# Order of the last two gate/value chunks of each batch in a fused attention and GeGLU kernel

## The chip, the cores and the metric

The kernel runs on one core of a Trainium2 chip. The metric is the device time of one execution in microseconds (us); lower is better. The time before is the median of three runs, 366.04 us (366.04 to 366.19). Matmuls run on TensorE (PE in the profile; its weight loads are PEld), elementwise work on VectorE (DVE), activation functions on ScalarE (ACT), masks and most DMA issues on GpSimd (POOL), and the stores and DMA transposes are issued by SyncE (SP). Matmul results land in PSUM[...].

## The reference: what is computed

In outline: causal attention over 8 batches, 8 heads, 576 positions and 64 dimensions, with 16 "beacon" keys that every position sees; its output, with the heads side by side, goes through a gated feed-forward block.

```python
k_all = np.concatenate([beacon_k, k], axis=2)          # 16 + 576 keys
scores = scale * np.matmul(q, k_all.transpose(0, 1, 3, 2))
scores = np.where(causal, -1e9, scores)
a = softmax(scores)
x = np.matmul(a, v_all)                                # -> x[4608, 512]
g, val = x @ w_gate, x @ w_val                         # 512 -> 1536
out = (gelu(g) * val) @ w_out                          # 1536 -> 512
```

Inputs and output are float32; the kernel computes in bfloat16 with float32 accumulation.

## The kernel before

The work is written out by hand, in program order, as one loop over the batches `b`. The feed-forward block works on chunks of 512 rows of x; chunk `b` is computed in the pass of batch `b`, and there are nine chunks, the ninth after the loop. Every engine runs its instructions in the order in which they are written.

A pass of batch `b` has two stages. In the **attention stage** the kernel computes scores of batch `b` in pieces, `scores(b, (m, c), ...)` with `m` the pair of heads and `c` one of four pieces of the triangle of keys and queries; each call fills one PSUM buffer, then ACT takes the exponential of it into SBUF, and POOL zeroes the masked corner (L320). `av` and `av_head` multiply the exponentials by v, `normalize` divides on DVE. Between these, `o(n)` puts the next `n` units of the output product of chunk `b-1`. For `b` above 1 the first twelve units are `out_half_mms`: each unit is two matmuls of 64 contraction rows, on the two halves of the array, into two banks, and after the twelfth DVE copies one bank (L471) and adds the other (L472). The rest are `out_mms`, one matmul of 128 rows each, and one copy (L469) per twelve.

In the **gate/value stage** there are twelve pairs `fi`: four matmuls of 512 columns for the gate, four for the value, Gelu on ACT from the gate's bank into `ge_sb` (L171), and a product on DVE of `ge_sb` and the value's bank into `hT_sb` (L448). The output product of the next pass reads `hT_sb`. All matmuls are recorded at one line, L168, all activations at L171, so the trace tells them apart by tile: `gv_ps`, `g_ps` and `v_ps` for gates and values, `s_ps` for scores, `o_ps` for outputs, `x_ps` for attention times v.

PSUM is divided among three pools: `psum_s` has three buffers of two banks each, used in turn; `psum_t` and `psum_o` have one bank each. A pair `fi` takes one `psum_s` buffer, gate in one bank and value in the other. The last pair of a batch (`fi` = 11, for `b` below 7) is split: its gate is put in `psum_t`, Gelu follows it at once, and its value has a `psum_s` buffer. A score call takes the next `psum_s` buffer, so the first three score calls of a pass take the buffers of the pairs 9, 10 and 11 of the pass before, each when its DVE product is done. The two banks of the half output product are `psum_t` and `psum_o`. In batch 0, after the pairs 4, 6 and 8, `transpose_wide` transposes q and k of batch 1 on PE: k through `psum_t`, from which DVE copies (L218, then L222), and q through `psum_o`, from which ACT copies.

ACT switches its function tables twice per pass: the load before the exponentials stands at L616, the one before Gelu at L655.

Of the kernel before, what the change touches and what calls it, by code (L numbers as in the profile page):

```python
# [7 lines left out]
P = 128  # L8
B, H, S, NB, D = 8, 8, 576, 16, 64
# [4 lines left out]
F_TILES = D_FF // P  # L14
K_CHUNKS = D_MODEL // P
CH = 512
# [24 lines left out]
FP32 = mybir.dt.float32  # L41
BF16 = mybir.dt.bfloat16
ACT = mybir.ActivationFunctionType
ALU = mybir.AluOpType
# [5 lines left out]
def kernel(  # L50
# [12 lines left out]
    nc = tc.nc  # L63
    keep = tc.keep_in_program_order
# [6 lines left out]
    fpool = ctx.enter_context(tc.tile_pool(name="fpool", bufs=3))  # L71
    hpool = ctx.enter_context(tc.tile_pool(name="hpool", bufs=2))
    opool = ctx.enter_context(tc.tile_pool(name="opool", bufs=2))
    psum_s = ctx.enter_context(tc.tile_pool(name="psum_s", bufs=3, space=bass.MemoryType.PSUM))
    psum_t = ctx.enter_context(tc.tile_pool(name="psum_t", bufs=1, space=bass.MemoryType.PSUM))
    psum_o = ctx.enter_context(tc.tile_pool(name="psum_o", bufs=1, space=bass.MemoryType.PSUM))
# [6 lines left out]
    wg_sb = const.tile([P, K_CHUNKS, D_FF], BF16, name="wg_sb", tag="wg_sb")  # L83
    wv_sb = const.tile([P, K_CHUNKS, D_FF], BF16, name="wv_sb", tag="wv_sb")
    wo_sb = const.tile([P, F_TILES, D_MODEL], BF16, name="wo_sb", tag="wo_sb")
    xT_sb = const.tile([P, NPAIR, N_TOK + P - KROWS[4]], BF16, name="xT_sb", tag="xT_sb")
# [80 lines left out]
    def mm(out_ap, lhsT, rhs, start, stop, **kw):  # L167
        keep(nc.tensor.matmul(out_ap, lhsT, rhs, start=start, stop=stop, **kw))  # L168

    def act(out_ap, in_ap, func, **kw):  # L170
        keep(nc.scalar.activation(out_ap, in_ap, func, **kw))  # L171
# [17 lines left out]
    def transpose_pe(b, m, by_act=False):  # L189
        t_ps = psum_s.tile([P, 2, 1024], BF16, name="t_ps", tag="s")  # L190
        for w in range(2):
            tr_part(b, m, w, t_ps[:, w, :])
        out_ap = qkT[:, m, :, NB:SK].rearrange("p w (t r) -> p w t r", r=6)
        in_ap = t_ps[:, 0:2, 0:S].rearrange("p w (r t) -> p w t r", r=6)
        keep(nc.vector.tensor_copy(out_ap[:, 1], in_ap[:, 1]))
        if by_act:
            act(out_ap[:, 0], in_ap[:, 0], ACT.Copy)
        else:
            keep(nc.vector.tensor_copy(out_ap[:, 0], in_ap[:, 0]))
        keep(nc.vector.tensor_copy(qkT[:, m, 1, 0:NB], t_ps[:, 1, S:SK]))  # L200
# [59 lines left out]
    def scores(b, *parts):  # L260
        s_ps = psum_s.tile([P, 2, 512], FP32, name="s_ps", tag="s")
        c0 = 0
        for m, c in parts:
            score_mms(b, m, c, s_ps[:, :, c0 : c0 + CHUNK_W[c]])
            c0 += CHUNK_W[c]
        (m, c), n = parts[0], len(parts)
        o, w = CHUNK_OFF[c], CHUNK_W[c]
        act(
            exp_ring[:, m : m + n, :, o : o + w].rearrange("p g h c -> p h g c"),
            s_ps[:, :, 0 : n * w].rearrange("p h (g c) -> p h g c", g=n),  # L270
            ACT.Exp,
            scale=QK_SCALE,
        )
        if b:
            for m, c in parts:
                masks(b, m, c)
# [87 lines left out]
    def av(b, m):  # L364
        x = psum_s.tile([P, 2, 512], FP32, name="x_ps", tag="s")
        for hi in range(2):
            attend(b, m, hi, x[:, hi, :])
        normalize(b, m, x, 0, 2)

    def av_head(b, m, hi, pool, tag):  # L370
        x = pool.tile([P, 1, 512], FP32, name="x_ps", tag=tag)
        attend(b, m, hi, x[:, 0, :])
        normalize(b, m, x, hi, hi + 1)
# [10 lines left out]
    def turn_dma(b, m):  # L384
        y_sb, y_before = y_of[b * NPAIR + m], y_of.pop((b - 1) * NPAIR + m)
        keep(nc.vector.tensor_copy(y_sb[0:NB, 0, :, :], y_before[KROWS[4] - NB : KROWS[4], 4, :, :]))
        c0 = b * S - NB
        keep(
            nc.sync.dma_start_transpose(
                out=xT_sb[:, m, c0 : c0 + 5 * P].rearrange("p (j n) -> p j n", n=P),  # L390
                in_=y_sb.rearrange("p j e d -> p (j e d)"),
            )
        )
# [3 lines left out]
    def hold(b, m):  # L397
        x = xT_sb[:, m, b * S : (b + 1) * S]
        keep(nc.gpsimd.tensor_copy(hold_sb, x[:, 0 : S : S - 1]))  # L399
# [9 lines left out]
    h_of, o_of = {}, {}  # L409

    gv_of = {}

    def gv_mms(ci, fi, *kks, split=False, last=False):
        if (ci, fi) not in gv_of:
            if split:
                gv_of[ci, fi] = (
                    psum_t.tile([P, CH], FP32, name="g_ps", tag="t"),
                    psum_s.tile([P, 2, CH], FP32, name="v_ps", tag="s")[:, 0, :],
                )
            else:  # L420
                gv_ps = psum_s.tile([P, 2, CH], FP32, name="gv_ps", tag="s")
                gv_of[ci, fi] = (gv_ps[:, 0, :], gv_ps[:, 1, :])
        n0 = ci * CH

        def part(w):
            for kk in kks:
                mm(
                    gv_of[ci, fi][w],
                    (wg_sb, wv_sb)[w][:, kk, fi * P : (fi + 1) * P],
                    xT_sb[:, kk, n0 : n0 + CH],  # L430
                    kk == 0,
                    last and kk == kks[-1],
                    skip_group_check=True,
                )

        part(0)
        if not split:
            part(1)
        if not last:
            return  # L440
        ge_sb = fpool.tile([P, CH], BF16, name="ge_sb", tag="ge_sb")
        act(ge_sb, gv_of[ci, fi][0], ACT.Gelu)
        if split:
            part(1)
        if ci not in h_of:
            h_of[ci] = hpool.tile([P, F_TILES, CH], BF16, name="hT_sb", tag="hT_sb")
        keep(
            nc.vector.tensor_tensor(  # L448
                out=h_of[ci][:, fi, :], in0=gv_of.pop((ci, fi))[1], in1=ge_sb, op=ALU.mult
            )  # L450
        )

    def gate_val(ci, fi, split=False):
        gv_mms(ci, fi, *range(K_CHUNKS), split=split, last=True)

    def out_mm(ci, ti, fi, o_ps, c0=0, c1=D_MODEL):
        mm(
# [47 lines left out]
    def out_mms(ci, u0, u1):  # L505
        for u in range(u0, u1):
# [19 lines left out]
            out=eye,  # L526
# [25 lines left out]
    def ahead(n):  # L552
        for load in loads[:n]:
            load()
        del loads[:n]
# [52 lines left out]
    for b in range(B):  # L608
        u = [0]

        def o(n, halves=False):
            (out_half_mms if halves else out_mms)(b - 1, u[0], u[0] + n)
            u[0] += n

        if b:
            keep(nc.scalar.preload_act_table_set(SET_EXP))  # L616
            o(3, b > 1)
            scores(b, (0, 0))
            scores(b, (0, 2))
            scores(b, (0, 1))  # L620
            o(5 if b == 1 else 9, b > 1)
            if b == 1:
                transpose_pe(1, 3)
                o(5)
            ahead(2)
            scores(b, (0, 3), (1, 3))
            scores(b, (1, 0))
            scores(b, (1, 2))
            ahead(2)
            o(5 if b == 1 else 6)  # L630
            av_head(b, 0, 0, psum_t, "t")
            o(1)
            scores(b, (1, 1))
            scores(b, (2, 0))
            scores(b, (2, 2))
            ahead(2)
            av_head(b, 0, 1, psum_t, "t")
            turn_dma(b, 0)
            o(7)
            scores(b, (2, 1))  # L640
            scores(b, (2, 3), (3, 3))
            scores(b, (3, 0))
            av_head(b, 1, 0, psum_o, "o")
            o(5)
            av_head(b, 1, 1, psum_o, "o")
            turn_dma(b, 1)
            scores(b, (3, 1))
            scores(b, (3, 2))
            av(b, 2)
            turn_dma(b, 2)  # L650
            o(6)
            av(b, 3)
            turn_dma(b, 3)
            o(11)
            keep(nc.scalar.preload_act_table_set(SET_GELU))  # L655
            for kk in range(K_CHUNKS):
                for fi in range(2):
                    gv_mms(b, fi, kk, last=kk == 3)
        for fi in range(F_TILES):
            if fi >= 2:  # L660
                gate_val(b, fi, fi == F_TILES - 1 and b < B - 1)
            if b == 0 and fi in (4, 6, 8):
                transpose_wide(1, (fi - 4) // 2)
            if fi == 0:
                if b and b + 1 < B:
                    hold(b, 3)
                    load_v(b + 1)
                if b and b + 2 < B:
                    load_qk(b + 2)
                if 2 <= b + 1 < B:  # L670
                    transpose_dma(b + 1)
                store(nc.sync)
# [40 lines left out]
```

The softmax here doesn't subtract the row's maximum and nothing guards it: scores larger than these inputs give would overflow.

## Time and profile before

| | |
|---|---|
| median of three runs | 366.04 us |
| profiled execution: its time | 365.93 us |
| profiled execution: its span | 364.1 us |
| PE busy | 353.7 us, 97% of the span |
| ACT busy | 192.7 us, 53% |
| DVE busy | 162.8 us, 45% |
| POOL busy | 161.2 us, 44% |
| mean time of a 512-column matmul as recorded | 379 ns |

The span is what the trace covers; the execution's time has some 1.8 us around it. Matmuls overlap in the array, so a matmul recorded with 379 ns doesn't hold PE for that long: four of them of the kind `g_ps` start at 161.95 us and the next four at 162.82 us, a step of about 0.216 us. What a matmul costs is therefore read from the starts of those beside it. In the timeline, each row is a run of like instructions on one engine: start, length in us, engine, line, operation, tiles, shapes and count, and in brackets how long the engine stood idle ahead of it and what ended that.

The passes of the batches 2 to 6 repeat every 38.94 us (the `g_ps` matmuls start at 84.22, 123.17, 162.12, 201.06 in the chain).

### The profile page before, as it was taken

What the parts mean: (1) busy time and instruction counts of PE and PEld (TensorE: products, weight loads), DVE (VectorE), ACT (ScalarE), POOL (GpSimd) and SP (SyncE); (2) the same over time, 40 slices, a digit from 0 to 9 for tenths busy, and PEclk for the clock granted to TensorE, in tenths of its full rate; (3) what the DMA queues carried; (4) which work ended last, traced back from release to release, by engine and by line L of the source; (5) the groups of instructions that cost most, each with busy time, mean ns of one, the idle gap of its engine ahead of it and who ended that gap; (6) DMA issues with size and microseconds to landing.
All of it is one profiled execution on the core that took longest, in us unless ns stands there. A gap on an engine that the chain in (4) does not pass through costs nothing.

```text
span 364.1 us, 7726 instructions
## 1 busy us (share of the span) xinstructions
PE 353.7 (97%) x3164; PEld 184.8 (51%) x3206; DVE 162.8 (45%) x320; ACT 192.7 (53%) x252; POOL 161.2 (44%) x288
## 2 busy tenths in 40 slices
PE   7899999999999999999999999999999999999996
PEld 6665446444654455445644464446544564444443
DVE  4547836344443345434534354334444453333332
ACT  3975788237923594349623891379335953321210
POOL 8934497655537552945375455565330530000000
DMA  7999999899179945999299917991797253000102
GB/s 105 173 203 204 198 126 99 129 170 188 23 126 147 215 45 76 163 215 64 56 148 221 111 38 121 170 198 27 112 136 136 17 60 115 0 2 29 58 36 110
DMA packets 160419, 41.57 MB, mean 114 GB/s; under 512 B 146944, under 2 KB 155904, under 8 KB 160384
## 3 DMA queue, kind: packets, MB, share of 16 engines
q0 software_dynamic: 104848, 19.11, 68.9%
q1 hardware_dynamic: 55536, 21.96, 30.7%
q8 instruction: 25, 0.41, 0.5%
q14 instruction: 10, 0.08, 0.1%
HBM read 38.27 MB, written 9.44 MB: 131 GB/s over the span
## 4 chain that ended last, share of the span: by engine, by line
PE 80%; DMA 8%; POOL 6%; ACT 3%; issue 2%; DVE 0%; ACTq 0%; POOLq 0%
PE gv_ps L168 42%; PE o_ps L168 21%; PE x_ps L168 8%; PE s_ps L168 6%; DMA wo_sb<-in_moe_w_out_dram 4%; DMA qk<-in_q_dram 4%; ACT expT L171 3%; POOL qk L111 1%; PE g_ps L168 1%; PE v_ps L168 1%; POOL v_sb L111 1%; POOL q_sb L111 1%; POOL wg_sb L111 1%; POOL wv_sb L111 1%; POOL expT L320 1%
## 5 line engine op out<-in xcount | busy, mean ns | idle before, releaser
L171 ACT ACTIVATE ge_sb<-gv_ps 128x512 bf16<-128x512 f32 x101 | 59.4, 597 | 141.8 <-PE gv_ps L168 139.5
L448 DVE TENSOR_TENSOR hT_sb<-gv_ps,ge_sb 128x512 bf16<-128x512 f32 x101 | 69.0, 691 | 111.6 <-ACT ge_sb L171 109.2
L168 PE MATMUL gv_ps<-xT_sb,wg_sb 128*128 128x512 bf16 x402 | 111.2, 379 | 0.5
L168 PE MATMUL gv_ps<-xT_sb,wv_sb 128*128 128x512 bf16 x388 | 107.9, 379 | 0.4
L171 ACT ACTIVATE expT<-s_ps 128x992 bf16<-128x992 f32 (+3 forms) x112 | 100.2, 979 | 7.0 <-PE s_ps L168 6.4
L168 PE MATMUL o_ps<-wo_sb,hT_sb 128*128 128x512 bf16 (+3 forms) x492 | 101.0, 373 | 1.3
L320 POOL TENSOR_SCALAR_AFFINE_SELECT expT<-expT 128x256 bf16<-128x256 bf16 (+1 forms) x140 | 52.2, 391 | 51.2 <-ACT expT L171 50.0
L168 PEld LDWEIGHTS <-wv_sb 128*128 128x128 bf16 x432 | 42.3, 98 | 50.6
L168 PEld LDWEIGHTS <-wg_sb 128*128 128x128 bf16 x432 | 42.1, 98 | 49.9
L168 PEld LDWEIGHTS <-hT_sb 128*128 128x128 bf16 (+1 forms) x516 | 39.5, 97 | 42.4 <-issue 4.1
L168 PEld LDWEIGHTS <-expT 128*128 128x128 bf16 (+1 forms) x960 | 33.6, 97 | 10.0 <-DVE y_sb L356 3.1
L168 PE MATMUL x_ps<-v_sb,expT 128*128 128x65 bf16 (+1 forms) x960 | 37.4, 193 | 0.2 <-POOL expT L320 0.2
L168 PE MATMUL s_ps<-qkT 64*128 64x80 bf16 (+5 forms) x528 | 33.6, 250 | 3.4 <-DVE qkT L239 1.6
L111 POOL DMA_DIRECT2D v_sb<-in_v_dram x40 | 33.6, 859 | 6.0 <-DMA wg_sb<-in_moe_w_gate_dram 1.8
L111 POOL DMA_DIRECT2D k_sb<-in_k_dram x30 | 25.2, 844 | 15.4 <-DMA q_sb<-in_q_dram 10.8
L356 DVE TENSOR_TENSOR y_sb<-x_ps,r_sb 128x320 bf16<-128x320 f32 (+1 forms) x47 | 28.8, 612 | 1.6
L111 POOL DMA_DIRECT2D q_sb<-in_q_dram x30 | 25.3, 879 | 6.4 <-DMA wo_sb<-in_moe_w_out_dram 3.5
L469 DVE COPY o_sb<-o_ps 128x512 f32<-128x512 f32 (+2 forms) x31 | 20.7, 668 | 15.3 <-PE o_ps L168 14.2
L354 DVE RECIPROCAL r_sb<-x_ps 128x5 f32<-128x5 f32 (+1 forms) x47 | 9.6, 204 | 39.1 <-PE x_ps L168 39.1
L168 PEld LDWEIGHTS <-qkT 64*128 64x128 bf16 x528 | 18.1, 95 | 17.2 <-issue 8.9
L399 POOL COPY hold_sb<-xT_sb 128x2 bf16<-128x2 bf16 x6 | 1.1, 186 | 30.8 <-DMA xT_sb<-y_sb 30.8
L471 DVE COPY o_sb<-o_ps 128x512 f32<-128x512 f32 x6 | 4.1, 691 | 15.4 <-PE o_ps L168 15.4
(58 smaller groups left out, 137.9 us busy)
## 6 DMA issues: line engine op xcount, KB each, us to landing
out_dram<-o_sb SPq DMA_DIRECT2D x35, 256.0 KB, 7.0
v_sb<-in_v_dram POOLq DMA_DIRECT2D x24, 128.0 KB, 9.0
q_sb<-in_q_dram POOLq DMA_DIRECT2D x18, 128.0 KB, 12.2
k_sb<-in_k_dram POOLq DMA_DIRECT2D x18, 128.0 KB, 5.8
wo_sb<-in_moe_w_out_dram POOLq DMA_DIRECT2D x3, 512.0 KB, 14.4
wg_sb<-in_moe_w_gate_dram POOLq DMA_DIRECT2D x2, 512.0 KB, 11.9
wv_sb<-in_moe_w_val_dram POOLq DMA_DIRECT2D x2, 512.0 KB, 13.5
v_sb<-in_v_dram POOLq DMA_DIRECT2D x8, 112.0 KB, 5.4
```

The source lines that it names most:

```text
L111: keep(nc.gpsimd.dma_start(out=out_ap, in_=in_ap))
L168: keep(nc.tensor.matmul(out_ap, lhsT, rhs, start=start, stop=stop, **kw))
L171: keep(nc.scalar.activation(out_ap, in_ap, func, **kw))
L320: nc.gpsimd.affine_select(out=d, in_=d, pattern=[[0, 2], [1, n]], compare_op=ALU.is_ge, fill=0.0, base=0, channel_multiplier=-1,)
L354: keep(nc.vector.reciprocal(r, x[:, :, :, D:DV]))
L356: nc.vector.tensor_tensor(out=y_of[i][:, :, h0:h1, :].rearrange("p j b d -> p b j d"), in0=x[:, :, :, 0:D], in1=r.to_broadcast([P, h1 - h0 ...
L399: keep(nc.gpsimd.tensor_copy(hold_sb, x[:, 0 : S : S - 1]))
L448: nc.vector.tensor_tensor(out=h_of[ci][:, fi, :], in0=gv_of.pop((ci, fi))[1], in1=ge_sb, op=ALU.mult)
L469: keep(nc.vector.tensor_copy(o_ap, o_ps))
L471: keep(nc.vector.tensor_copy(o_ap, o_half))
```

## The change

The last two pairs of a batch, 10 and 11, are now taken together for `b` below 7: gate 10 into `psum_t`, Gelu, gate 11 into `psum_o`, Gelu, then value 10 into a `psum_s` buffer, product, value 11 into the next `psum_s` buffer, product. And in the next pass the first output units ahead of the scores are one instead of three; the two that are left out there come after the third score call (for `b` = 1 in the second of the two groups after it). The helper that did both forms is taken apart into `part`, `gelu` and `gated`. No instruction is added or dropped on any engine.

```diff
-    def gv_mms(ci, fi, *kks, split=False, last=False):
-        ...
+    def part(ci, fi, w, ps, kks=range(K_CHUNKS), last=True):
         n0 = ci * CH
-        ...
+        for kk in kks:
+            mm(
+                ps,
+                (wg_sb, wv_sb)[w][:, kk, fi * P : (fi + 1) * P],
+                xT_sb[:, kk, n0 : n0 + CH],
+                kk == 0,
+                last and kk == kks[-1],
+                skip_group_check=True,
+            )
+
+    def gelu(g_ps):
         ge_sb = fpool.tile([P, CH], BF16, name="ge_sb", tag="ge_sb")
-        act(ge_sb, gv_of[ci, fi][0], ACT.Gelu)
-        if split:
-            part(1)
+        act(ge_sb, g_ps, ACT.Gelu)
+        return ge_sb
+
+    def gated(ci, fi, v_ps, ge_sb):
         if ci not in h_of:
             h_of[ci] = hpool.tile([P, F_TILES, CH], BF16, name="hT_sb", tag="hT_sb")
-        ...
+        keep(nc.vector.tensor_tensor(out=h_of[ci][:, fi, :], in0=v_ps, in1=ge_sb, op=ALU.mult))
+
+    ...
+    def gates_first(ci, *fis):
+        ge_of = {}
+        for fi, (pool, tag) in zip(fis, ((psum_t, "t"), (psum_o, "o"))):
+            g_ps = pool.tile([P, CH], FP32, name="g_ps", tag=tag)
+            part(ci, fi, 0, g_ps)
+            ge_of[fi] = gelu(g_ps)
+        for fi in fis:
+            v_ps = psum_s.tile([P, 2, CH], FP32, name="v_ps", tag="s")[:, 0, :]
+            part(ci, fi, 1, v_ps)
+            gated(ci, fi, v_ps, ge_of[fi])
...
             keep(nc.scalar.preload_act_table_set(SET_EXP))
-            o(3, b > 1)
+            o(1, b > 1)
             scores(b, (0, 0))
             scores(b, (0, 2))
             scores(b, (0, 1))
-            o(5 if b == 1 else 9, b > 1)
+            o(5 if b == 1 else 11, b > 1)
             if b == 1:
                 transpose_pe(1, 3)
-                o(5)
+                o(7)
...
         for fi in range(F_TILES):
-            if fi >= 2:
-                gate_val(b, fi, fi == F_TILES - 1 and b < B - 1)
+            if fi >= 2 and (fi < F_TILES - 2 or b == B - 1):
+                gate_val(b, fi)
+            if fi == F_TILES - 2 and b < B - 1:
+                gates_first(b, fi, fi + 1)
             if b == 0 and fi in (4, 6, 8):
                 transpose_wide(1, (fi - 4) // 2)
```

More of the change, by code (lines that the diff above doesn't have):

```diff
@@ L411 @@
     gv_of = {}
-    def gv_mms(ci, fi, *kks, split=False, last=False):
-        if (ci, fi) not in gv_of:
-            if split:
[L416 to L422, printed above, removed]
-        n0 = ci * CH
[L425 to L437, printed above, removed]
-            part(1)
-        if not last:
-            return
+    def part(ci, fi, w, ps, kks=range(K_CHUNKS), last=True):
+        n0 = ci * CH
+        for kk in kks:
[7 more added lines that the diff above has]
+            )
@@ L441, in gv_mms @@
+    def gelu(g_ps):
         ge_sb = fpool.tile([P, CH], BF16, name="ge_sb", tag="ge_sb")
-        act(ge_sb, gv_of[ci, fi][0], ACT.Gelu)
-        if split:
-            part(1)
+        act(ge_sb, g_ps, ACT.Gelu)
+        return ge_sb
+    def gated(ci, fi, v_ps, ge_sb):
         if ci not in h_of:
             h_of[ci] = hpool.tile([P, F_TILES, CH], BF16, name="hT_sb", tag="hT_sb")
[L447 to L451, printed above, removed]
@@ L453, in gate_val, with gv_mms @@
-    def gate_val(ci, fi, split=False):
-        gv_mms(ci, fi, *range(K_CHUNKS), split=split, last=True)
+        keep(nc.vector.tensor_tensor(out=h_of[ci][:, fi, :], in0=v_ps, in1=ge_sb, op=ALU.mult))
+    def gv_mms(ci, fi, *kks, last=False):
+        if (ci, fi) not in gv_of:
+            gv_of[ci, fi] = psum_s.tile([P, 2, CH], FP32, name="gv_ps", tag="s")
+        gv_ps = gv_of[ci, fi]
+        for w in range(2):
+            part(ci, fi, w, gv_ps[:, w, :], kks, last)
+        if last:
+            gated(ci, fi, gv_ps[:, 1, :], gelu(gv_ps[:, 0, :]))
@@ new lines, in gate_val @@
+    def gate_val(ci, fi):
+        gv_mms(ci, fi, *range(K_CHUNKS), last=True)
+    def gates_first(ci, *fis):
[8 more added lines that the diff above has]
+            gated(ci, fi, v_ps, ge_of[fi])
```

## The prediction

> **What bounds the kernel now.** I read the page's head and its chain first, then the list of waits, then the timeline around two batch boundaries. The page and the list of waits:
>
> ```profile
> span 364.1 us, 7726 instructions
> ...
> PE 353.7 (97%) x3164; PEld 184.8 (51%) x3206; DVE 162.8 (45%) x320; ACT 192.7 (53%) x252; POOL 161.2 (44%) x288
> ```
>
> ```profile
> PE s_ps L168 <- ACT expT L171: 0.9, 6, 0.2
> ```
>
> PE sets the end, and the rows of PE in the list of waits add up to under 5 us. The change adds and drops no instruction, so it can only move PE's standing still. The only repeated wait of PE is one per boundary from batch 2 on (6 times), for an exponential. The timeline of the boundary between batches 3 and 4:
>
> ```profile
> 161.95 1.03 PE L168 MATMUL g_ps<-xT_sb,wg_sb 128*128 128x512 bf16 x4
> 162.15 0.60 ACT L171 ACTIVATE ge_sb<-gv_ps 128x512 bf16<-128x512 f32 x1 [1.13 <-PE gv_ps L168]
> ...
> 162.82 1.03 PE L168 MATMUL v_ps<-xT_sb,wv_sb 128*128 128x512 bf16 x4
> 163.02 0.60 ACT L171 ACTIVATE ge_sb<-g_ps 128x512 bf16<-128x512 f32 x1 [0.27 <-PE g_ps L168]
> 163.63 1.28 ACT L616 ACT_TABLE_LOAD   x1
> 163.78 0.82 PE L168 MATMUL o_ps<-wo_sb,hT_sb 64*128 64x512 bf16 x6
> 163.95 0.69 DVE L448 TENSOR_TENSOR hT_sb<-v_ps,ge_sb 128x512 bf16<-128x512 f32 x1 [0.48 <-PE v_ps L168]
> 164.43 0.80 PE L168 MATMUL s_ps<-qkT 64*128 64x512 bf16 x14
> ...
> 165.06 2.11 PE L168 MATMUL o_ps<-wo_sb,hT_sb 64*128 64x512 bf16 x18
> ...
> 167.01 0.56 PE L168 MATMUL s_ps<-qkT 64*128 64x128 bf16 x10
> 167.21 0.69 DVE L471 COPY o_sb<-o_ps 128x512 f32<-128x512 f32 x1 [2.57 <-PE o_ps L168]
> 167.72 0.37 PE L168 MATMUL s_ps<-qkT 64*128 64x384 bf16 x4 [0.15 <-ACT expT L171]
> ...
> 168.03 0.39 PE L168 MATMUL o_ps<-wo_sb,hT_sb 128*128 128x512 bf16 x1
> ```
>
> To see: the table load ends at 164.91 us, when the first scores are ready, so the exponentials start late; the score call (1,2) at 167.72 waits for the third of them. And there are two near misses. The product of pair 11 ends at 163.95 + 0.69 = 164.64, just ahead of the third score call, which takes its buffer; and the copy L471 ends at 167.90, just ahead of the `o_ps` matmuls at 168.03, which take its bank. The boundary between batches 0 and 1:
>
> ```profile
> 41.34 1.95 DVE L218 COPY qkT<-t_ps 64x288 bf16<-64x288 bf16 x4
> ...
> 42.36 1.03 PE L168 MATMUL gv_ps<-xT_sb,wg_sb 128*128 128x512 bf16 x4
> ...
> 43.30 0.17 DVE L222 COPY qkT<-t_ps 128x16 bf16<-128x16 bf16 x1
> ```
>
> To see: DVE empties `psum_t` of the transposed keys until 43.47 us, while gate 10 starts at 42.36. Today gate 10 doesn't need that bank; gate 11 does, at 44.09.
>
> **What the skill says.** "PSUM — Partial Sum Buffer", section "PSUM bank collisions raise a hardware error", has PSUM guarded bank by bank, not by address: so gate 10 must await the last small copy L222 too. "Perfetto Trace Analysis", section "Optimizing Tensor Performance", advises rotating matmul groups through banks so that evacuation overlaps the next group; the trace agrees, and the question is which rotation comes up short. "ScalarE: Activation LUTs", section "What ACT_TABLE_LOAD costs", gives about 1283 ns for the load; the trace has 1.28 us. It adds some 1380 ns for a drain; here the exponential starts right after the load, so the trace's 1.28 is used alone.
>
> **Unit costs, from starts.** 512 columns: 0.216 us (161.95 to 162.82 is four); three pairs of 64-row matmuls, 163.78 to 164.43, are 0.65, so a half unit is also 0.216. Scores (0,2) with 464 columns, 0.20; (0,1) with 496, 0.21; these two run from 164.65 to 165.06. From 128-row to 64-row work and back PE loses 0.10 (162.82 + 4 × 0.216 = 163.68, seen 163.78). From the end of a DVE instruction to the PE work that it releases: 0.05 (copy L200 ends 50.66 + 0.16 = 50.82; the weights that wait for it load at 50.87).
>
> **Boundaries of batches 2 to 7 (six).** Gates and values are the same sixteen matmuls, so the first half unit still starts at 163.78.
> - Removed: two half units ahead of the scores, −0.43. (0,0) starts at 164.00, (0,2) at 164.22, and (0,1) could at 164.41. ACT: Gelu 11 follows gate 11 at 162.15, the table is there at 162.77 + 1.28 = 164.05. Exponentials then start when the scores are ready: (0,0) began at 164.43 today, and ACT's wait for such a matmul takes 0.38 + 0.10, so 164.48 instead of 164.92, 0.44 sooner. Moving the Gelus costs nothing: ACT is idle 1.13 us ahead of each.
> - Added: (0,1) takes the bank of value 11. Value 11 ends when it did, and its product, released by PE, still runs 163.95 to 164.64 (product 10 now waits for value 10, about 163.09 to 163.78, and is out of the way; (0,2) is not held). So (0,1) starts at 164.70, not 164.41: +0.29. Behind it in PE's queue is everything.
> - Moved: eleven half units from 164.91 to 164.91 + 11 × 0.216 = 167.29, today 167.01: +0.28.
> - Won: (1,2) follows (0,3) and (1,0), 0.18 + 0.22, at 167.69; its exponential is done at 167.67 − 0.44 = 167.23. Today it could have started at 167.41 and did at 167.72: −0.31.
> - Late next: the copy L471 follows the last half unit by 0.20 and takes 0.69: 167.49 to 168.18. The full units need its bank: 168.24. PE is there at 167.69 + 0.21 + 0.10 = 168.00 and stands for 0.24.
>
> Sum: 168.24 − 168.03 = +0.21. Everything after it (masks, attention, normalisation) is paced by PE and shifts alike, as do the DMA transposes; the loads have their slack. Six times: **+1.26 us**. Ends: if the change of row mode comes after the wait and not under it, +0.31; if the copy doesn't hold the full units, −0.03.
>
> **Boundary of batches 0 and 1.**
> - Gate 10 waits for L222: 43.47 + 0.06 = 43.53 instead of 42.36: **+1.17**. Gate 11 takes `psum_o`, emptied by ACT at 42.82: free.
> - Two full units fewer ahead of the scores: −0.43. The wait of (0,1) for product 11: +0.29. The two units come back in the second group: +0.43. Today's wait of (1,2) for the DVE copies of `transpose_pe` (about 0.06) goes: −0.06.
> - Absorbed: attention of batch 1 stands still today because POOL has its masks behind DMA issues:
>
> ```profile
> 52.27 0.44 PE L168 MATMUL x_ps<-v_sb,expT 128*128 128x65 bf16 x9
> ...
> 52.88 0.24 PE L168 MATMUL x_ps<-v_sb,expT 128*128 128x65 bf16 x2 [0.17 <-POOL expT L320]
> ```
>
> Nine matmuls of about 0.03 end at 52.54; the next starts at 52.88, so 0.34 is lost. POOL's DMA issues there are not paced by PE, so with PE 1.4 later the mask is ready: −0.34.
>
> Sum +1.06, between +0.7 (more is absorbed in POOL's queue) and +1.4 (nothing is).
>
> **In all** +1.26 + 1.06 = +2.3 us. The profiled execution, 365.93 us with span 364.1, would become some 368.2 with 366.4; it lies 0.1 under the median, 366.04, which becomes 368.4.
>
> **Rivals.**
> 1. The copy L471 doesn't hold the full units (for: today it hardly does, 0.07 of slack; against: it starts with the last half unit, which comes 0.28 later). Six times −0.03, with +1.06: 366.9. Chance 0.10.
> 2. Batch 1 absorbs most of the stall, since POOL's queue, not PE, paces its first attention (for: the row above; against: after 52.88 I find no further wait of PE there). 1.26 + 0.2: 367.5. Chance 0.08.
> 3. The other side: (0,1) doesn't wait for product 11, so the earlier exponentials pay. Its place is the third score call, its price 0.29 at each of seven boundaries; it decides at 164.36, the latest end of that product that doesn't hold (0,1). Then (1,2) starts at 167.41, and only the copy, ending 167.90, holds the full units to 167.96: −0.07 six times; batch 0 has 1.06 − 0.29 = 0.77: +0.3, 366.4. Against: buffers are used in turn, and nothing makes product 11 end sooner. Chance 0.07.
>
> **How the numbers follow.** The main case has 0.75, and its own range, 367.6 to 369.3, comes from 0.7 + 6 × 0.15 and 1.4 + 6 × 0.31. To leave out no more than 2 in 10, the range is taken from 367.2, which holds rival 2, to 369.3. Within 0.2% (0.73 us, about what a measurement of this kernel can tell from no change) lie most of rival 3 and the low edge of rival 1: 0.07. Faster needs rival 3 with the batch 0 stall absorbed too: 0.02. Slower: 0.91.
>
> **What the profile after would show.** In the waits of PE: `g_ps` waiting for DVE L222 once, about 1.2 us; `s_ps` waiting for the product of `v_ps` seven times, about 0.3 in the starts (less as listed, since recorded matmuls overlap); `o_ps` waiting for the L471 copy's new line six times; no more `s_ps` for `expT`. The period of the passes goes from 38.94 to 39.15 us; the first exponentials start 0.44 sooner relative to gate 10. Wrong would be: `g_ps` of batch 0 starting at 42.4; a period of 38.9 (rivals 1 and 3); an attention of batch 1 that starts less than 1 us later than today.

## The result, and the profile after

The kernel after takes 368.21 us (median of 6 runs, 367.71 to 368.75), the kernel before 366.04 us (365.61 to 366.19, 6 runs). The ratio is 1.0062, 95% interval [1.0049, 1.0075]: 0.62% slower, some 2.2 us. The forecast was 368.4 us, in a range of 367.2 to 369.3.

The profiled execution of the kernel after took 368.49 us, with this span and these busy times:

```profile
span 366.7 us, 7733 instructions
...
PE 354.7 (97%) x3164; PEld 187.3 (51%) x3206; DVE 162.9 (44%) x320; ACT 193.2 (53%) x252; POOL 161.2 (44%) x288
```

The counts by engine are those of before; the seven instructions that were added after all (7733 against 7726) are waits for semaphores on DVE, 60 where there were 53. The span is 2.6 us longer, with DVE and POOL as they were. PE's busy time, 1.0 us higher for the same matmuls, hides some of that: a recorded matmul lasts longer than the step to the next one, so a short stall can lie under it. PE stands still for longer, and the list of its waits in the kernel after says where (engine, line, what it waited for; total us, times, longest):

```profile
PE o_ps L168 <- DVE o_sb L473: 1.1, 6, 0.2
PE g_ps L168 <- DVE qkT L222: 1.0, 1, 1.0
```

The wait of `s_ps` for the exponential is gone from the list, as forecast, and two new ones are there: the full output units wait for the copy of the half product at six boundaries, and gate 10 of batch 0 waits once for the last copy out of `psum_t`. A third row that was forecast, `s_ps` waiting for the product of value 11 seven times, isn't there: that stall is real, but it has to be read from the starts of the matmuls, as is done below. The timeline of the boundary 0 to 1 shows the wait of gate 10:

```profile
43.31 0.17 DVE L222 COPY qkT<-t_ps 128x16 bf16<-128x16 bf16 x1
...
43.53 1.90 PE L168 MATMUL g_ps<-xT_sb,wg_sb 128*128 128x512 bf16 x8 [0.99 <-DVE qkT L222]
```

Gate 10 starts at 43.53 us, the number that the prediction gave, against 42.36 before. The timeline of the boundary 3 to 4 after the change:

```profile
163.68 1.89 PE L168 MATMUL v_ps<-xT_sb,wv_sb 128*128 128x512 bf16 x8
...
164.50 1.28 ACT L618 ACT_TABLE_LOAD   x1
...
165.50 0.39 PE L168 MATMUL o_ps<-wo_sb,hT_sb 64*128 64x512 bf16 x2
165.68 0.69 DVE L433 TENSOR_TENSOR hT_sb<-v_ps,ge_sb 128x512 bf16<-128x512 f32 x1 [0.17 <-PE v_ps L168]
165.73 1.09 PE L168 MATMUL s_ps<-qkT 64*128 64x512 bf16 x14
166.21 2.75 ACT L171 ACTIVATE expT<-s_ps 128x1024 bf16<-128x1024 f32 x3 [0.43 <-PE s_ps L168]
166.64 2.55 PE L168 MATMUL o_ps<-wo_sb,hT_sb 64*128 64x512 bf16 x22
...
169.23 0.69 DVE L473 COPY o_sb<-o_ps 128x512 f32<-128x512 f32 x1 [2.86 <-PE o_ps L168]
...
169.97 0.38 PE L168 MATMUL o_ps<-wo_sb,hT_sb 128*128 128x512 bf16 x1 [0.18 <-DVE o_sb L473]
```

Three rows carry it. The fourteen score matmuls of the first burst now span 1.09 us, where they spanned 0.80. The last matmuls of the second call start at 166.11 and the first of the third at 166.42; at the usual step it would have been 166.14. So the third call stands 0.28 us, until the product of value 11 is done at 165.68 + 0.69 = 166.37. As the matmul at 166.11 is recorded with 0.20 us, only 0.12 us look idle, and the list of waits has no stretch under 0.15. The exponentials do start earlier, 0.71 us after the first half unit against 1.14 before (163.78 to 164.92). And that gain ends at the copy: from 169.23 to 169.92, with the full units at 169.97, 4.47 us after the first half unit against 4.25 before.

The chain of the kernel after has gate 10 of the batches 1 and 2 at

```profile
83.82 1.73 PE g_ps L168 x8
122.97 1.73 PE g_ps L168 x8
```

so a pass takes 39.15 us, where it took 38.95. Following one fixed piece of work through both traces, the first attention matmul of the batches 1 to 7, the lag grows like this (starts of the `x_ps` matmuls, us):

| batch | before | after | lag |
|---|---|---|---|
| 1 | 52.27 | 53.66 | 1.40 |
| 2 | 91.44 | 92.97 | 1.53 |
| 3 | 130.39 | 132.12 | 1.73 |
| 4 | 169.34 | 171.26 | 1.93 |
| 5 | 208.29 | 210.41 | 2.13 |
| 6 | 247.24 | 249.56 | 2.33 |
| 7 | 286.19 | 288.72 | 2.53 |

Six boundaries cost 0.20 us each, 1.2 together, and boundary 0 to 1 the other 1.33. The first row of the table says 1.40 because the lag still changes within the pass of batch 1: it falls to 1.06 at the tenth of its attention matmuls and rises to 1.32 at the seventieth (why is said with the prediction, below). Nothing of the start is in it: the attention matmul of batch 0 at 19.79 us before starts at 19.80 after.

### The profile page after: what moved, and what is told of

Its sections match the earlier page's. It is cut to its first block, busy times and chain, and to the rows that moved or that the text cites. A ratio compares the mean times of both kernels' runs of the same rounds, so it can differ in the third digit from the quotient of the medians.

```text
span 366.7 us, 7733 instructions
## 1 busy us (share of the span) xinstructions
PE 354.7 (97%) x3164; PEld 187.3 (51%) x3206; DVE 162.9 (44%) x320; ACT 193.2 (53%) x252; POOL 161.2 (44%) x288
## 4 chain that ended last, share of the span: by engine, by line
PE 83%; DMA 5%; DVE 5%; POOL 3%; issue 1%; ACT 1%; DVEq 0%; SPq 0%; POOLq 0%
PE gv_ps L168 39%; PE o_ps L168 23%; PE x_ps L168 8%; PE s_ps L168 5%; DMA q_sb<-in_q_dram 3%; PE g_ps L168 3%; PE v_ps L168 3%; PE t_ps L176 2%; DVE hT_sb L433 1%; DMA k_sb<-in_k_dram 1%; POOL v_sb L111 1%; DVE qkT L235 1%; POOL k_sb L111 1%; PE w_ps L168 1%; DVE o_sb L473 1%
## 5 line engine op out<-in xcount | busy, mean ns | idle before, releaser
L171 ACT ACTIVATE ge_sb<-gv_ps 128x512 bf16<-128x512 f32 x94 | 55.3, 597 | 134.4 <-PE gv_ps L168 132.1
L433 DVE TENSOR_TENSOR hT_sb<-gv_ps,ge_sb 128x512 bf16<-128x512 f32 x94 | 64.2, 691 | 104.6 <-ACT ge_sb L171 104.6
L168 PE MATMUL gv_ps<-xT_sb,wg_sb 128*128 128x512 bf16 x374 | 104.1, 379 | 0.5
L168 PE MATMUL gv_ps<-xT_sb,wv_sb 128*128 128x512 bf16 x360 | 100.7, 379 | 0.4
L168 PEld LDWEIGHTS <-hT_sb 128*128 128x128 bf16 (+1 forms) x516 | 41.3, 96 | 43.5 <-issue 5.2
L433 DVE TENSOR_TENSOR hT_sb<-v_ps,ge_sb 128x512 bf16<-128x512 f32 x14 | 9.7, 692 | 11.5 <-PE v_ps L168 11.5
```

What stands on the lines that cost most here:

```text
L433: keep(nc.vector.tensor_tensor(out=h_of[ci][:, fi, :], in0=v_ps, in1=ge_sb, op=ALU.mult))
```

## The experiments

**Theory**: two separate costs. Gate 10 of batch 0 comes before DVE has emptied its bank; and the earlier score burst runs into the bank of value 11, which delays the half product, its copy and the full units behind it. **Rivals**: the new order of gates and values itself slows each boundary; or the copy is no limit; or the stall of batch 0 is absorbed. The first four kernels shared their runs of the kernel before (365.77 us, 19 runs), and so did the last four (365.73 us, 9 runs). A whole time or span has the start of the execution in it, which differs: that attention matmul of batch 0, at 19.79 us before, starts between 18.94 and 20.38 in the ten traces. Periods of the passes are free of that and tell more. So does the stretch from that matmul to the first attention matmul of batch 2, which takes in the boundaries 0 to 1 and 1 to 2: 71.65 us before the change, 73.17 after, 1.52 more, of which 0.20 is boundary 1 to 2.

### Gates first alone

```diff
-            o(1, b > 1)
+            o(3, b > 1)
...
-            o(5 if b == 1 else 11, b > 1)
+            o(5 if b == 1 else 9, b > 1)
...
-                o(7)
+                o(5)
```

> Gates first as in the change, but three output units ahead of the first scores as before. Theory (each part has its own cost: gate 10 of batch 0 waits for psum_t; the earlier score burst runs into the bank of value 11): the boundaries of batches 2 to 7 cost nothing, period 38.94 us, since the first scores are ready at 164.91 as before, when the table is long there, so the exponentials gain nothing; boundary 0 to 1 costs 1.17 less what POOL's queue absorbs, about +0.8 to +1.1. In all about 367.0 us. Rival (the new order itself slows every boundary, for example by the later product 10): about 368.2 us, period 39.15.

Measured: 366.57 us, ratio 1.0024 [1.0013, 1.0035]; its passes take 38.94 us, as before the change. Only boundary 0 to 1 costs:

```profile
PE g_ps L168 <- DVE qkT L222: 1.0, 1, 1.0
```

The new order costs nothing at the other boundaries, and by itself wins nothing there: in its timeline the exponentials start at 165.58, 1.14 us after the first half unit at 164.44, as before. The first scores had come no sooner. The stretch from batch 0 to batch 2 is 1.00 us longer than before the change.

### Earlier scores alone

```diff
-            o(3, b > 1)
+            o(1, b > 1)
...
-            o(5 if b == 1 else 9, b > 1)
+            o(5 if b == 1 else 11, b > 1)
...
-                o(5)
+                o(7)
```

(to the kernel before)

> The old order of gates and values, but one output unit ahead of the first scores instead of three. Theory: the third score call waits about 0.28 us for the product of value 11, and the half output product ends 0.28 later, so do its copy and the full units behind it: period 39.15 as with the whole change (+0.20 each), though the exponentials here still start at the table load's end. Batch 0 doesn't wait for psum_t, boundary 0 to 1 about 0. In all about 367.2 us. Rival (the loss per boundary comes from gates first): period 38.94, 366.0 us.

Measured: 367.27 us, ratio 1.0046 [1.0034, 1.0059], and gate 11 in its chain:

```profile
124.09 0.86 PE g_ps L168 x4
...
163.24 0.86 PE g_ps L168 x4
```

A period of 39.15 us: the whole loss per boundary with none of the gain. The timeline of the same kernel has the score burst and the release of the full units as in the whole change:

```profile
165.12 1.09 PE L168 MATMUL s_ps<-qkT 64*128 64x512 bf16 x14
166.03 2.55 PE L168 MATMUL o_ps<-wo_sb,hT_sb 64*128 64x512 bf16 x22
...
168.62 0.69 DVE L471 COPY o_sb<-o_ps 128x512 f32<-128x512 f32 x1 [2.86 <-PE o_ps L168]
...
169.37 0.81 PE L168 MATMUL o_ps<-wo_sb,hT_sb 128*128 128x512 bf16 x3
```

The exponentials' 0.44 us make no difference, since the copy decides either way. The two halves of the change add up: 0.24% and 0.46%, against 0.62% for both.

### Batch 0 as before

```diff
-            if fi >= 2 and (fi < F_TILES - 2 or b == B - 1):
+            if fi >= 2 and (fi < F_TILES - 2 or b == B - 1 or (b == 0 and fi == F_TILES - 2)):
                 gate_val(b, fi)
+            if b == 0 and fi == F_TILES - 1:
+                split_pair(b, fi)
-            if fi == F_TILES - 2 and b < B - 1:
+            if fi == F_TILES - 2 and 0 < b < B - 1:
                 gates_first(b, fi, fi + 1)
```

(`split_pair` does pair 11 as before the change: gate in `psum_t`, Gelu, value, product)

> The whole change, but batch 0 keeps the old order of its last two pairs. Theory: the wait of gate 10 for psum_t of 1.2 us is gone, boundary 0 to 1 costs about 0 instead of 1.3; the period stays 39.15. About 367.2 us with a span some 1.3 under that of the change. Rival (the stall of batch 0 is absorbed elsewhere in batch 1): within 0.3 us of the change, 368 us.

Measured: 367.04 us, ratio 1.0044 [1.0030, 1.0057]; gate 10 of successive batches at 120.99, 160.14, 199.29 in its chain, a period of 39.15 us. The wait of `g_ps` for L222 is not in its list of waits. What is left is the six boundaries and little else: the stretch from batch 0 to batch 2 is 0.34 us longer than before the change, against 1.52 with the whole change, and 0.20 of the 0.34 is boundary 1 to 2. By time alone, the step from the whole change (1.0062) is no larger than the uncertainty of the two; the waits, the period and this stretch are what decide. So the stall of batch 0 isn't absorbed.

### The third score call two half units later

Batches 0 and 1 as before the change (that part of the edit isn't shown); from batch 2 on

```diff
...
-            o(1, b > 1)
+            o(3 if b == 1 else 1, b > 1)
             scores(b, (0, 0))
             scores(b, (0, 2))
+            if b > 1:
+                o(2, True)
             scores(b, (0, 1))
-            o(5 if b == 1 else 11, b > 1)
+            o(5 if b == 1 else 9, b > 1)
...
```

> Gates first from batch 1 on, batch 0 and the pass of batch 1 as before; from batch 2 on one half unit, two score calls, two half units, the third score call, nine half units. Theory: the third call comes at about 164.85, after product 11, so nothing waits for it; exponentials start 0.44 sooner; the wait for the third exponential (0.31) is gone, but the full units then wait for the copy of the half product, so only 0.07 of it is won: period 38.87, about 365.6 us. Rival (the copy is no limit): the full 0.31 is won at six boundaries, period 38.63, 364.1 us. Other rival (something else holds the third call): period 39.15, 367.2 us.

Measured: 365.33 us against 365.77, ratio 0.9988 [0.9980, 0.9996], a little faster than before the change. Its chain and its waits:

```profile
121.70 1.73 PE g_ps L168 x8
...
160.56 1.73 PE g_ps L168 x8
```

```profile
PE o_ps L168 <- DVE o_sb L481: 1.1, 6, 0.2
```

The period is 38.86 us, 0.09 under the kernel before. With nothing in the way of the third call the earlier exponentials are a gain, of which the copy lets through 0.09 of 0.31.

### Batch 0 with the banks exchanged

```diff
-        for fi, (pool, tag) in zip(fis, ((psum_t, "t"), (psum_o, "o"))):
+        for fi, (pool, tag) in zip(fis, ((psum_t, "t"), (psum_o, "o"))[:: 1 if ci else -1]):
```

(to the whole change)

> The whole change, but in batch 0 gate 10 is put in psum_o and gate 11 in psum_t. Theory (gate 10 waits for whoever empties its bank): ACT empties psum_o at about 42.82, so gate 10 starts at about 42.88, 0.65 sooner than with the change, and gate 11 no longer waits for psum_t. Period stays 39.15. About 0.4 to 0.65 us under the change: 1.5 to 2.1 us over the kernel before. Rival (batch 1 takes the stall up anyway): same as the change, 2.2 to 2.5 over the kernel before.

Measured: 367.54 us, 1.8 us over the 365.73 of before, ratio 1.0047 [1.0035, 1.0060]; the period stays 39.15 us (82.90, 122.05, 161.20). The wait has moved to the engine that empties the other bank, and is shorter. The list of waits:

```profile
PE g_ps L168 <- ACT qkT L171: 0.3, 1, 0.3
```

In the starts of the matmuls PE stands 0.51 us here, against 1.16 with the whole change. The stretch from batch 0 to batch 2 is 0.88 us longer than before the change, 0.63 less than with the whole change. A bank that is emptied 0.65 us sooner makes the stall smaller by as much, as the theory has it.

### A short copy

To the kernel with the third call later:

```diff
-            keep(nc.vector.tensor_copy(o_ap, o_half))
-            keep(nc.vector.tensor_tensor(out=o_ap, in0=o_ps, in1=o_ap, op=ALU.add))
+            l_ap, r_ap = o_ap[:, 0:128], o_ap[:, 128:D_MODEL]
+            keep(nc.vector.tensor_copy(l_ap, o_half[:, 0:128]))
+            keep(nc.vector.tensor_tensor(out=l_ap, in0=o_ps[:, 0:128], in1=l_ap, op=ALU.add))
+            keep(nc.vector.tensor_copy(r_ap, o_ps[:, 128:D_MODEL]))
```

> As the kernel with the third call later, but only 128 of the 512 columns of the second half product are copied and added; for the other columns the first half product is stored alone, so that a quarter to a half of the contraction is left out of them. Theory (the copy of the second half product holds the full units): the bank is free some 0.4 us sooner, the full units follow the scores at once, period 38.63 (0.31 under the kernel before), 1.9 us under the kernel before in all. Rival (something else holds the full units): period 38.86, 0.4 us under the kernel before.

Measured: 364.17 us, ratio 0.9955 [0.9943, 0.9968], 1.6 us under the kernel before; gate 10 at 120.96 and 159.58, a period of 38.62 us. That is less than the 1.9 us expected, as two passes are longer, 38.85 and 38.73 us (on the first of them see the end of the text; the second stays open). In its timeline the copy takes 0.29 us and the full units no longer wait for it:

```profile
282.60 0.29 DVE L482 COPY o_sb<-o_ps 128x128 f32<-128x128 f32 x1 [2.57 <-PE o_ps L168]
...
283.09 1.47 PE L168 MATMUL o_ps<-wo_sb,hT_sb 128*128 128x512 bf16 x6
```

So the copy was the limit: shortening it releases the rest of the 0.31 us. The sum behind it is shorter too, but it reads the other bank, and the full units ask for the one that the copy empties.

### The last half unit as one full unit, behind the scores

Most of that gain, in a kernel that leaves nothing out. In the half product, units 0 to 10 stay half units, the copy follows unit 10, and unit 11 is one matmul of 128 rows into the first bank, put after the score calls:

```diff
...
+            if fi == F_TILES - 1:
+                mm(halves[0], h_of[ci][:, fi, 0:P], wo_sb[:, fi, :], False, True, skip_group_check=True)
+                keep(nc.vector.tensor_tensor(out=o_ap, in0=halves[0], in1=o_ap, op=ALU.add))
+                ...
...
-            if fi == F_TILES - 1:
-                out_store(ci, 0, halves[0], o_half=halves[1])
+            if fi == F_TILES - 2:
+                keep(nc.vector.tensor_copy(o_ap, halves[1]))
...
-            o(5 if b == 1 else 9, b > 1)
+            o(5 if b == 1 else 8, b > 1)
...
             scores(b, (1, 2))
             ahead(2)
+            if b > 1:
+                o(1, True)
             o(5 if b == 1 else 6)
```

> As the kernel with the third call later, but the twelfth half unit is left out of the burst and put after the score call (1,2) as one full matmul of 128 rows into the first bank; the copy of the second bank follows the eleventh. Theory: the copy starts 0.22 sooner and has 0.22 more work of PE beside it, so nothing waits for it; (1,2) comes 0.22 sooner and waits about 0.09 for the third exponential. Period 38.72 (0.22 under the kernel before), 1.3 us under it in all. Rival (a full matmul after half ones into one bank, or the later sum, costs more than it wins): period 38.86 or more, 0.4 us under the kernel before or less.

Measured: 364.58 us, ratio 0.9967 [0.9955, 0.9980]; gate 10 at 82.05, 120.77 and 159.49, a period of 38.72 us, as worked out. One pass takes 38.87 us (see the end of the text).

### No half unit ahead of the scores

And with the scores right behind value 11:

```diff
-            o(3 if b == 1 else 1, b > 1)
+            if b == 1:
+                o(3)
             scores(b, (0, 0))
             scores(b, (0, 2))
             if b > 1:
-                o(2, True)
+                o(3, True)
             scores(b, (0, 1))
```

> As the kernel with the last unit full, but no half unit ahead of the first two score calls and three between the second and the third. Theory: exponentials start another 0.22 sooner, (1,2) no longer waits, period 38.63 (0.31 under the kernel before), 1.9 us under it in all. Rival (the second score call waits for product 10, or the table load for Gelu 11 now sets the start): period 38.72 or more.

Measured: 363.96 us, ratio 0.9951 [0.9938, 0.9965]: 1.8 us under the kernel before and faster than both kernels. Gate 10 stands at 81.80 and 120.45 in its chain, a period of 38.65 us; one pass takes 38.87 us (see the end of the text). The boundary 6 to 7 in its timeline:

```profile
278.82 0.69 DVE L433 TENSOR_TENSOR hT_sb<-v_ps,ge_sb 128x512 bf16<-128x512 f32 x1 [0.17 <-PE v_ps L168]
...
279.14 2.75 ACT L171 ACTIVATE expT<-s_ps 128x1024 bf16<-128x1024 f32 x3 [0.22 <-PE s_ps L168]
279.72 0.38 PE L168 MATMUL s_ps<-qkT 64*128 64x80 bf16 x8
...
281.87 0.69 DVE L519 COPY o_sb<-o_ps 128x512 f32<-128x512 f32 x1 [2.36 <-PE o_ps L168]
...
282.36 1.71 PE L168 MATMUL o_ps<-wo_sb,hT_sb 128*128 128x512 bf16 x7
```

The product of value 11 ends at 279.51, and the third call comes at 279.72. The copy ends at 282.56, while unit 11 into the other bank holds PE until about then. Every bank is free just before it is asked for; what is left of the copy's wait is some 0.04 us.

## Why the prediction was right

It held in time, and step by step but for one term, what the pass of batch 1 absorbs.

- **Gate 10 of batch 0**: +1.17 worked out, start at 43.53 us; seen: 43.53 us. The list of waits names the last, small copy L222, and with the banks exchanged the wait went with the bank. That agrees with the Trainium skill, "PSUM — Partial Sum Buffer", section "PSUM bank collisions raise a hardware error", which has PSUM guarded by bank and not by address, but it doesn't test that rule: the 512 float32 columns of gate 10 are a whole bank here (a `psum_s` buffer of two banks is two times 512), so they cover the columns that L222 reads, and by address too gate 10 would have had to wait.
- **The third score call**: +0.29 worked out; 0.28 us in the starts, at all seven boundaries, though not in the list of waits, where the prediction looked for it too. Earlier scores alone showed it without the new order of gates, and with the third call later it is gone.
- **The exponentials**: 0.44 sooner worked out; 0.43 seen (0.71 against 1.14 us after the first half unit). Their wait is gone. Rival 3, on the other side, needed the third call not to wait; it was false of the change, but moving that call showed that its mechanism exists.
- **The copy**: +0.21 per boundary worked out; 0.20 seen, six times. Rival 1, that the copy holds nothing, is out: the wait is listed six times, and the short copy took it away.
- **Boundary 0 to 1**: +1.06 worked out; +1.33 seen. The size that was off is what POOL's queue absorbs. Up to the first attention of batch 1 the terms give 1.17 − 0.43 + 0.29 + 0.43 − 0.06 = 1.40, and 1.40 is seen. The 0.34 us there was absorbed: the lag falls to 1.06, and that attention, two rows with a wait before, is now one unbroken row in the timeline:

```profile
53.66 0.62 PE L168 MATMUL x_ps<-v_sb,expT 128*128 128x65 bf16 x15
```

  But later in the same pass the weights of the attention of batch 1 wait for another mask, some 0.24 us in the starts, and the lag is 1.32 again:

```profile
61.15 0.23 PEld L168 LDWEIGHTS <-expT 128*128 128x128 bf16 x6 [0.19 <-POOL expT L320]
```

  The step that said "after 52.88 I find no further wait of PE there" held for the trace before and not for this one. The ten traces show more: each has one of the two stalls and never both. The kernel before, the third call later and the last unit full have the first (0.34 to 0.76 us) and not the second; the other seven have the second (about 0.2 us) and not the first. Among these seven are the short copy and the last kernel, whose code is as before the change up to this place, so PE's lateness isn't shown to be what removed the first stall. Its going, on which the −0.34 rested, may be luck; what isn't in the prediction is that the other stall then comes, so that some 0.1 us was to be won and not 0.34. Rival 2, that most of the stall is absorbed, is out: the stretch from batch 0 to batch 2 is 1.52 us longer, and 0.34 when batch 0 keeps its old order.

By the traces the two sums are 1.2 + 1.33 = 2.5 us, against the 2.3 of the prediction. That the medians, 2.2 us apart, come as close lies within their spread (367.71 to 368.75 for the kernel after) and is no merit of the prediction.

## What to carry to other kernels

An order that starts work sooner pays only as far as the next buffer in its path lets it: before moving a burst forward, work out for each buffer that it takes when the last reader lets go, and then follow the delay to the next buffer after that. A wait that shows in the profile can hide a second one right behind it; here the listed wait for an exponential stood 0.07 us ahead of a copy, so that removing it won 0.09 and not 0.31. Here moving only the call that needs the bank, and giving PE work that needs another bank, turned the loss into a gain. And a stall can be too short for a list of waits and still cost its 0.28 us at every boundary: compare the starts.

## What was not expected of the hardware

In three of the kernels (the short copy, the last unit full, no unit ahead), at the boundary before batch 4 alone, the DVE product of value 11 began about 0.43 us after the start of the semaphore wait ahead of it in DVE's queue, where it is 0.065 us at the other boundaries of these kernels. Two rows of the last kernel's timeline show that product there and at the next boundary, with DVE's idle time before it:

```profile
163.03 0.69 DVE L433 TENSOR_TENSOR hT_sb<-v_ps,ge_sb 128x512 bf16<-128x512 f32 x1 [0.54 <-PE s_ps L168]
...
201.53 0.69 DVE L433 TENSOR_TENSOR hT_sb<-v_ps,ge_sb 128x512 bf16<-128x512 f32 x1 [0.17 <-PE v_ps L168]
```

The third score call waits for that product, and the pass is 0.15 to 0.24 us longer than its neighbours. By the trace the inputs were there.

What the three have in common is a place in DVE's queue: the late product is the 192nd instruction of DVE in each of these traces (semaphore waits counted). In the other five kernels with the new order of gates the 192nd is a semaphore wait, and it too starts 0.36 to 0.38 us later behind its predecessor than the same instruction of the other passes; there no stall of PE follows from it. The 320th of DVE is late as well, by 0.21 to 0.38 us, in the five of these kernels where it can be told. On ACT the 320th, an exponential, starts 0.34 to 0.36 us behind its predecessor in all ten kernels, where the same one of other passes takes 0.06 to 0.15. So the delay goes with the place in the queue, whatever instruction stands there, and between the two places lie 128 instructions. What happens there isn't shown.

The change of PE between 128-row and 64-row matmuls, in either direction, cost 0.095 to 0.106 us in the starts each time in the kernel before and in the last one, also where no wait was near. In the kernel after it lay within the wait for the copy at the six boundaries.
